# Strassen products in layer 1 of the last two groups, a later start for batch 1's loads, and a written order in place of a list scheduler

## The chip, the cores, the metric

One core of one Trainium2 chip. Times are device microseconds (us) of one execution. The kernel before takes 303.9 us (median of 3 runs, 302.27 to 304.15). It was run again beside every experiment, so each result also has a ratio to runs of the kernel before on the same chip in the same minutes. Runs marked slow (four of experiments, eight of the kernel before, all of these beside c1 to c3) are left out of ratios.

## The reference

Linear attention with cosine weights (8 batches, 8 heads, 576 tokens, head size 64), then a feed-forward part on all 4608 tokens whose gate is h cos h:

```python
def phi(x, c, s):
    r = np.maximum(x, 0.0)
    return np.concatenate([r * c, r * s], axis=-1)
q_p, k_p = phi(q, cos_w, sin_w), phi(k, cos_w, sin_w)
kv = np.einsum('bhsf,bhsd->bhfd', k_p, v)
num = np.einsum('bhsf,bhfd->bhsd', q_p, kv)
den = np.einsum('bhsf,bhf->bhs', q_p, np.sum(k_p, axis=2))[..., None] + 1e-06
x = (num / den).transpose(0, 2, 1, 3).reshape(B * S, H * D)   # 4608 x 512
h = x @ w_in                                                  # 512 x 2048
out = (h * np.cos(h)) @ w_out                                 # 2048 x 512
```

## The kernel before

The 4608 tokens make nine groups of 512: batches 0 to 6, "r" (the fifth tiles of all batches), batch 7. A group goes through layer 1 (products with `w_in`, cosine on ScalarE, gate on VectorE) and layer 2 (products with `w_out`). Layer 2 of all groups but 0 uses Strassen's seven half-size products in place of eight. The kernel describes all work as operations with engines, assumed durations and buffers; a list scheduler orders them on assumed times, and each engine then gets a fixed list.

```python
SQ, DQ, LAND = "SP", "DMA", 2.0                      # assumed: a transfer lands 2.0 us late
def run(self, cold=0.0):                             # the list scheduler
    ...
        t0, e0 = min((c[0], c[1]) for c in cand)
        t, _, us, o, _ = min((c for c in cand if c[1] == e0 and c[0] <= t0 + self.EPS), key=...)
...
# batch 1's loads wait for two quarters of w_out
if b == 1:
    deps.append(w_land[NG + 1])
...
# layer 1, every group: plain, one bank per 512 columns, 4 matmuls of 512
ps[key] = ppool.tile([P, len(js), s1 - s0], F32, name="M1", tag="m1")
...
# layer 2, Strassen, groups 1 to 7 and r: three banks X, Y, Z, five additions on VectorE
e1 = op({"A": 0.6}, EV, lambda e: cp(e, part(g, "s1"), ps[(g, "X")]), deps=[p1], acq=[s1])
p6 = product(1, wsum, S_(1), [sY])
e6 = op({"V": 0.69}, EV, lambda e: add(part(g, "u2"), g, "Y", "s1"), deps=[p6, e1], ...)
...
# layer 2 of group 0: plain, 64 matmuls of 512
layer2_plain(lambda t, n: (1, 1, t, n))
```

The kernel uses eight banks of PSUM, the memory that TensorE's results go to: four in ring "m1", two in "l2", and one tile of two banks, "at", which attention uses for sums over all eight heads.

Names in the profile: `qm`, `km`, `vm` are inputs as loaded, `qp` and `kp` their features phi(q) and phi(k), `V` the values cast to 16 bits; `KV` and `N` are attention's products, `x` its result, `xT` and `TP` transposes; `M` is a bank of layer 1, `ch` the cosine, `g` the gated result; `PX`, `PY`, `PZ` are layer 2's banks X, Y, Z (in the kernel after Y is mostly called `SD`); `s`, `WT`, `WS` are Strassen's sums, `ost` the output.

Of the kernel before, what the change touches and what calls it, by code (L numbers as in the profile page):

```python
# [14 lines left out]

class Slot:


    def __init__(self, ring, n=1):
        self.ring, self.left, self.end = ring, n, 0.0  # L20


def flat(x):
    return tuple(z for y in x for z in flat(y)) if isinstance(x, tuple) else (x,)


class Op:
    def __init__(self, alts, prio, fn, deps, lat, acq, rel, at):
        self.alts, self.prio, self.fn, self.deps, self.lat = alts, flat(prio), fn, deps, lat
        self.acq, self.rel, self.at, self.end = acq, rel, at, None  # L30


class Plan:


    SEM, EPS = 0.08, 0.1

    def __init__(self, rings):
        self.ops, self.free = [], {r: [0.0] * n for r, n in rings.items()}
# [6 lines left out]
    def run(self, cold=0.0):  # L46
        users, wait = {}, {}
        for o in self.ops:
            wait[o] = len(o.deps)
            for d in o.deps:  # L50
                users.setdefault(d, []).append(o)
        ready = [o for o in self.ops if not wait[o]]
        clock, order = {}, []
        while ready:
            cand = []
            for o in ready:
                t = max([o.at] + [d.end + d.lat for d in o.deps])
                if any(not self.free[s.ring] for s in o.acq):
                    continue
                for s in o.acq:  # L60
                    t = max(t, min(self.free[s.ring]))
                for e, us in o.alts.items():
                    cand.append((max(t, clock.get(e, 0.0)), e, us, o, t))
            if not cand:
                left = [(o.prio, o.alts, [s.ring for s in o.acq if not self.free[s.ring]],
                         [(d.prio, d.alts) for d in o.deps if d.end is None][:3])
                        for o in self.ops if o.end is None]
                raise RuntimeError("no operation can start: " + repr(left[:12]))
            t0, e0 = min((c[0], c[1]) for c in cand)
            t, _, us, o, _ = min(  # L70
                (c for c in cand if c[1] == e0 and c[0] <= t0 + self.EPS),
                key=lambda c: (c[4] if e0 == "DMA" else 0.0, c[3].prio, c[0]))
            if e0 == "PE" and t < cold:
                us *= 1.7
            for s in o.acq:
                self.free[s.ring].remove(min(self.free[s.ring]))
            o.end = t + us + (self.SEM if us else 0.0)
            clock[e0] = t + us
            for s in o.rel:
                s.left, s.end = s.left - 1, max(s.end, o.end)  # L80
                if not s.left:
                    self.free[s.ring].append(s.end)
            order.append((t, len(order), o, e0))
            ready.remove(o)
            for u in users.get(o, ()):
                wait[u] -= 1
                if not wait[u]:
                    ready.append(u)
        assert len(order) == len(self.ops)
        order.sort(key=lambda x: x[:2])  # L90
        return [(o, e) for _, _, o, e in order]
# [3 lines left out]
def kernel(  # L95
# [50 lines left out]
    WT = cpool.tile([P, 4, HJ, HM], F16, name="WT")  # L146
# [4 lines left out]
    kvzs, kps, qps, qTs, qTr, x16s, xts, gts, sms, osts, ps = ({} for _ in range(11))  # L151
    T, T1 = range(NT), range(NT + 1)
    HS = [slice(0, HB), slice(HB, H)]
    RING = {"m1": 4, "l2": 2, "at": 1}
# [20 lines left out]
    def feat(eng, b, name, t, g, hs=ALLH):  # L175
        dst = (kps if name == "k" else qps)[b][:, t, hs, g, :]
        src, sc = raw[name][:, hs, t, :], CS[:, b % 2, g, t:t + 1]
        if eng == "A":
            nc.scalar.activation(out=dst, in_=src, func=AF.Relu, scale=sc)  # L179
        else:  # L180
            (nc.vector if eng == "V" else nc.gpsimd).tensor_scalar(  # L181
                out=dst, in0=src, scalar1=0.0, scalar2=sc, op0=ALU.max, op1=ALU.mult)
# [10 lines left out]
    def q_tiles(b):  # L193
        qps[b] = apool.tile([P, NT + 1, H, 2, D], F16, name=f"qp{b}", tag="qp", bufs=1)

    def qT_tiles(b):
        qTs[b] = apool.tile([P, NT, H, P], F16, name=f"qT{b}", tag="qT", bufs=1)

    def qR_tiles(b):
        qTr[b] = apool.tile([P, H, P], F16, name=f"qR{b}", tag="qR", bufs=2)  # L200

    def qT(b, t):
        return qTs[b][:, t] if t < NT else qTr[b]
# [27 lines left out]

    def ratio(b, t, tile_, hbs):
        nb, h0 = len(hbs), hbs[0] * HB
        den = apool.tile([P, nb, HB], F32, name=f"den{b}_{t}", tag="den")
        nc.vector.tensor_scalar_add(out=den, in0=tile_[:, :, :, D], scalar1=1e-6)
        rec = apool.tile([P, nb, HB], F32, name=f"rec{b}_{t}", tag="rec")
        nc.vector.reciprocal(out=rec, in_=den)  # L237
        if hbs[0] == 0:
            x16s[(b, t)] = apool.tile([P, H, D], F16, name=f"x16{b}_{t}", tag="x16", bufs=4)
# [19 lines left out]

    def transposes(key, tag, srcs_, **kw):  # L260
# [4 lines left out]
    def q_src(b, t, h):  # L265
        return qps[b][:, t, h].rearrange("p g d -> p (g d)")

    def q_trans_dma(b, t):
        nc.sync.dma_start_transpose(  # L269
            out=qT(b, t), in_=qps[b][:, t].rearrange("p h g d -> p (h g d)"))  # L270
# [12 lines left out]

    def sin(key):
        ps[("ch", key)] = apool.tile([P, SM], F32, name="ch", tag="ch", bufs=4)
# [4 lines left out]
    def gate(key, dst):  # L290
        m = ps[key]
        nc.vector.tensor_tensor(  # L292
            out=dst, in0=m, in1=ps[("ch", key)].rearrange("p (j s) -> p j s", s=m.shape[2]),
            op=ALU.mult)
# [4 lines left out]
    def s_tiles(g):  # L299
        sms[g] = gpool.tile([P, 2, HJ, HT], F16, name=f"s{g}", tag="s")  # L300

    def sums(g, c, n):
# [3 lines left out]
        a12, s1, s2 = gv[:, 1, js, 0:HT], sms[g][:, 0, js], sms[g][:, 1, js]  # L306
        out, in0, in1, op = ((s1, a21, a22, ALU.add), (s2, s1, a11, ALU.subtract),
                             (a21, a11, a21, ALU.subtract), (a12, a12, s2, ALU.subtract))[n]
        nc.vector.tensor_tensor(out=out, in0=in0, in1=in1, op=op)  # L309

    def weight_sum(n):
        wv = w_out_sb.rearrange("p (j e) m -> p e j m", e=2)
        b11, b12 = wv[:, 0, :, 0:HM], wv[:, 0, :, HM:Dm]
        b21, b22 = wv[:, 1, :, 0:HM], wv[:, 1, :, HM:Dm]
        x, y = ((b12, b11), (b22, WT[:, 0]), (b22, b12), (b21, WT[:, 1]))[n]
        nc.vector.tensor_tensor(out=WT[:, n], in0=x, in1=y, op=ALU.subtract)

    def prod(g, n, c):
        gv = gts[g].rearrange("p (j e) s -> p e j s", e=2)
        sv, wv = sms[g], w_out_sb.rearrange("p (j e) m -> p e j m", e=2)  # L320
        lo, hi, ml, mh = slice(0, HT), slice(HT, SM), slice(0, HM), slice(HM, Dm)
        bank, first, lhs, rhs = (
            ("X", True, gv[:, 0, :, lo], wv[:, 0, :, ml]),
            ("Y", True, sv[:, 1], WT[:, 1]),
            ("X", False, gv[:, 1, :, lo], wv[:, 1, :, ml]),
            ("Y", False, gv[:, 0, :, hi], WT[:, 2]),
            ("Z", True, sv[:, 0], WT[:, 0]),
            ("Y", False, gv[:, 1, :, hi], WT[:, 3]),
            ("Z", False, gv[:, 1, :, lo], wv[:, 1, :, mh]))[n]
        first = first and c == 0  # L330
        if first:
            tag = "m1" if bank == "Z" and g in ALONE else "l2"
            ps[(g, bank)] = ppool.tile(
                [P, 2, HM], F32, name=f"P{bank}", tag=tag, bufs=4 if tag == "m1" else 2)
        for i in range(2):
            for j in range(c * HJ // 2, (c + 1) * HJ // 2):
                nc.tensor.matmul(  # L337
                    ps[(g, bank)][:, i, :], lhsT=lhs[:, j, i * P:(i + 1) * P], rhs=rhs[:, j],
                    start=(first and i == 0 and j == 0), stop=(j == HJ - 1),
                    skip_group_check=True)  # L340

    def part(g, name):
        ps[(g, name)] = apool.tile([P, 2, HM], F32, name=name, tag=name, bufs=1)
# [6 lines left out]
    def add(dst, g, bank, other):  # L350
        nc.vector.tensor_tensor(out=dst, in0=ps[(g, bank)], in1=ps[(g, other)], op=ALU.add)  # L351

    def rows(b):
        ap = out[b * S:(b + 1) * S, :]
        return (ap[0:S5].rearrange("(p t) m -> p t m", t=NT + 1),
                ap[S5:S].rearrange("(p t) m -> p t m", t=NT))

# [13 lines left out]

    def plain2(t, js):
        if js[0] == 0:
            ps[("M2", t)] = ppool.tile([P, Dm], F32, name="M2", tag="l2", bufs=2)
        for j in js:
            nc.tensor.matmul(  # L376
                ps[("M2", t)], lhsT=gts[0][:, j, t * P:(t + 1) * P], rhs=w_out_sb[:, j, :],
                start=(j == 0), stop=(j == NJT - 1))
# [26 lines left out]
    def weights(n):  # L405
# [4 lines left out]
        else:  # L410
# [3 lines left out]
    plan = Plan({"m1": 4, "l2": 2, "at": 1, "raw_k": 1, "raw_q": 1, "raw_v": 1, "kp": 1,  # L414
                 "qp": 1, "V1": 1, "kvz": 3, "qT": 1, "qR": 2, "xT": 2, "x16": 4, "ch": 4,
                 "g": 2, "s": 2, "ld": 2, "s1": 1, "u2": 1, "u3": 1, "ost0": 1, "ost1": 1})
# [380 lines left out]
```

## Time and profile before

| | kernel before |
|---|---|
| time, median of 3 (us) | 303.9 |
| profiled run: its time, the span in its trace (us) | 300.7, 298.7 |
| TensorE, time that its matmuls need | 270.0 |
| holes 23.3 to 67 / 67 to 235 / 235 to end | 2.3 / 9.9 / 0.0 |
| first cosine of layer 1: batch 1 / r / batch 7 (us) | 59.7 / 230.5 / 256.5 |

How to read it: I count a **hole** from the trace's matmul records, as the time from one matmul's start to the next one's, less what the first needs when they stand back to back (216 ns for 512 columns, 109 for 256, 56 for 128, 30 for 65, as the records of the kernel before have them), if over 0.12 us. This is finer than length minus busy time, which the prediction uses: a matmul's record is 0.16 us longer than these spacings (379 ns for 512 columns, 273 for 256) and counts as busy to its end, so each hole looks shorter. "Time that matmuls need" is the recorded number of each size times those spacings. The profile's lines for the kernel before are in the prediction.

### The profile page before, as it was taken

What the parts mean: (1) busy time and instruction counts of PE and PEld (TensorE: products, weight loads), DVE (VectorE), ACT (ScalarE), POOL (GpSimd) and SP (SyncE); (2) the same over time, 40 slices, a digit from 0 to 9 for tenths busy, and PEclk for the clock granted to TensorE, in tenths of its full rate; (3) what the DMA queues carried; (4) which work ended last, traced back from release to release, by engine and by line L of the source; (5) the groups of instructions that cost most, each with busy time, mean ns of one, the idle gap of its engine ahead of it and who ended that gap; (6) DMA issues with size and microseconds to landing.
All of it is one profiled execution on the core that took longest, in us unless ns stands there. A gap on an engine that the chain in (4) does not pass through costs nothing.

```text
span 298.7 us, 6583 instructions
## 1 busy us (share of the span) xinstructions
PE 280.1 (94%) x2565; PEld 201.3 (67%) x2565; DVE 233.7 (78%) x450; ACT 175.6 (59%) x303; POOL 102.0 (34%) x107
## 2 busy tenths in 40 slices
PE   8879999899969987999979999999999999999993
PEld 8768856688855555566646666776666666566782
DVE  1878888899995798887869798987786786768661
ACT  2846748599379797679489497634433443443210
POOL 1370004396191686287077194011002001100500
PEclk9979999999999999999999999999999999999998
DMA  7799995897899999999999999715202100200213
GB/s 218 264 163 203 204 362 183 279 308 120 273 274 235 356 232 169 283 278 203 322 256 202 238 369 195 141 47 151 35 0 94 48 1 32 111 2 0 91 52 140
DMA packets 77086, 53.29 MB, mean 178 GB/s; under 512 B 46080, under 2 KB 74752, under 8 KB 77056
## 3 DMA queue, kind: packets, MB, share of 16 engines
q1 hardware_dynamic: 69760, 39.73, 55.2%
q0 software_dynamic: 6848, 12.59, 16.6%
q10 hardware_dynamic: 448, 0.57, 0.5%
q8 instruction: 20, 0.33, 0.5%
q14 instruction: 10, 0.08, 0.1%
HBM read 36.74 MB, written 9.44 MB: 155 GB/s over the span
## 4 chain that ended last, share of the span: by engine, by line
PE 55%; DMA 16%; DVE 10%; POOL 5%; SPq 5%; ACT 4%; issue 3%; ACTq 0%; DVEq 0%
PE M L279 26%; DMA vm<-in_v_dram 13%; PE PY L337 8%; PE PZ L337 6%; PE PX L337 5%; PE M L376 5%; POOL qp L181 4%; DMA qm<-in_q_dram 3%; PE KV L219 2%; DVE g L292 2%; SPq L171 2%; DVE x L241 2%; PE TP L263 2%; DVE s L309 2%; SPq L269 1%
## 5 line engine op out<-in xcount | busy, mean ns | idle before, releaser
L279 PE MATMUL M<-xT,w_in_sb 128*128 128x512 f16 (+1 forms) x640 | 120.2, 336 | 2.9 <-ACT xT L159 2.6
L286 ACT ACTIVATE ch<-M 128x512 f32<-128x512 f32 x144 | 84.9, 595 | 60.8 <-PE M L279 58.7
L292 DVE TENSOR_TENSOR g<-M,ch 128x512 f16<-128x512 f32 x128 | 85.8, 687 | 27.0 <-ACT ch L286 26.1
L279 PEld LDWEIGHTS <-w_in_sb 128*128 128x128 f16 x704 | 67.3, 98 | 46.6 <-issue 3.1
L181 POOL TENSOR_SCALAR qp<-qm,CS 128x512 f16<-128x512 f32 x29 | 60.0, 2074 | 31.0 <-DMA qm<-in_q_dram 27.0
L337 PEld LDWEIGHTS <-g 128*128 128x128 f16 x560 | 54.1, 98 | 11.5
L369 POOL DMA_DIRECT2D out_dram<-ost x14 | 7.8, 558 | 98.6 <-DVE ost L351 42.5
L179 ACT ACTIVATE kp<-km,CS 128x512 f16<-128x512 f32 x52 | 35.1, 715 | 0.2
L179 ACT ACTIVATE qp<-qm,CS 128x512 f16<-128x512 f32 x40 | 26.9, 713 | 11.9 <-DMA qm<-in_q_dram 11.9
L337 PE MATMUL PX<-w_out_sb,g 128*128 128x256 f16 x224 | 27.6, 273 | 0.0
L241 DVE TENSOR_TENSOR x<-N,rec 128x512 f16<-128x512 f32 (+1 forms) x44 | 26.1, 594 | 1.7 <-DVE rec L237 0.2
L337 PE MATMUL PY<-WT,g 128*128 128x256 f16 x224 | 27.2, 273 | 0.0
L337 PEld LDWEIGHTS <-s 128*128 128x128 f16 x224 | 21.4, 98 | 7.1 <-DVE s L309 2.8
L161 POOL CAST V<-vm 128x512 f16<-128x512 f32 (+1 forms) x22 | 13.9, 664 | 15.9 <-DMA vm<-in_v_dram 15.9
L228 PE MATMUL N<-kvz,qT 128*128 128x65 f16 x256 | 14.7, 196 | 2.3 <-DVE x L241 2.1
L228 PEld LDWEIGHTS <-qT 128*128 128x128 f16 x256 | 12.6, 100 | 6.1 <-issue 3.5
L337 PE MATMUL PY<-WT,s 128*128 128x256 f16 x112 | 14.1, 273 | 2.2 <-DVE s L309 2.2
L181 DVE TENSOR_SCALAR kp<-km,CS 128x512 f16<-128x512 f32 x28 | 15.5, 590 | 0.3 <-DMA km<-in_k_dram 0.2
L292 DVE TENSOR_TENSOR gr<-M,ch 128x512 f16<-128x512 f32 x16 | 10.9, 689 | 5.7 <-ACT ch L286 5.5
L219 PE MATMUL KV<-V,kp 128*128 128x65 f16 x320 | 12.9, 196 | 2.5 <-DVE kp L181 0.7
L279 PE MATMUL M<-xR,w_in_sb 128*128 128x512 f16 x64 | 15.1, 379 | 0.0
L219 PEld LDWEIGHTS <-kp 128*128 128x128 f16 x320 | 11.7, 99 | 4.7 <-issue 2.4
(70 smaller groups left out, 287.7 us busy)
## 6 DMA issues: line engine op xcount, KB each, us to landing
out_dram<-ost POOLq DMA_DIRECT2D x28, 256.0 KB, 4.1
qm<-in_q_dram SPq DMA_DIRECT2D x8, 640.0 KB, 5.3
km<-in_k_dram SPq DMA_DIRECT2D x8, 640.0 KB, 7.0
qm<-in_q_dram SPq DMA_DIRECT2D x8, 512.0 KB, 5.8
km<-in_k_dram SPq DMA_DIRECT2D x8, 512.0 KB, 8.8
vm<-in_v_dram SPq DMA_DIRECT2D x6, 640.0 KB, 8.1
vm<-in_v_dram SPq DMA_DIRECT2D x6, 512.0 KB, 8.9
w_in_sb<-in_moe_w_in_dram POOLq DMA_DIRECT2D x4, 512.0 KB, 9.0
```

What stands on the lines that cost most here:

```text
L161: (nc.vector if eng == "V" else nc.gpsimd).tensor_copy(out=out, in_=in_)
L179: nc.scalar.activation(out=dst, in_=src, func=AF.Relu, scale=sc)
L181: (nc.vector if eng == "V" else nc.gpsimd).tensor_scalar(out=dst, in0=src, scalar1=0.0, scalar2=sc, op0=ALU.max, op1=ALU.mult)
L219: nc.tensor.matmul(tile_[:, n, hh, :], lhsT=kps[b][:, t, h].rearrange("p g d -> p (g d)"), rhs=V1[:, t, h, :], start=(t == 0), stop=(t == NT))
L228: nc.tensor.matmul(tile_[:, n, hh, :], lhsT=qT(p, t)[:, h, :], rhs=kvzs[p][:, h, :], start=(i == 0), stop=(i == len(parts) - 1))
L241: nc.vector.tensor_tensor(out=dst, in0=tile_[:, :, :, 0:D], in1=rec.unsqueeze(3).broadcast_to((P, nb, HB, D)), op=ALU.mult)
L279: nc.tensor.matmul(ps[key][:, n, :], lhsT=w_in_sb[:, c, j * P:(j + 1) * P], rhs=x[:, c, s0:s1], start=(c == 0 and n == 0), stop=(c == NCT ...
L286: nc.scalar.activation(out=ps[("ch", key)], in_=ps[key].rearrange("p j s -> p (j s)"), func=AF.Sin, bias=math.pi / 2.0, scale=1.0)
L292: nc.vector.tensor_tensor(out=dst, in0=m, in1=ps[("ch", key)].rearrange("p (j s) -> p j s", s=m.shape[2]), op=ALU.mult)
L337: nc.tensor.matmul(ps[(g, bank)][:, i, :], lhsT=lhs[:, j, i * P:(i + 1) * P], rhs=rhs[:, j], start=(first and i == 0 and j == 0), stop=(j ...
L369: e0.dma_start(out=five[:, t0:t0 + 2, :], in_=blocks(ost, n))
L376: nc.tensor.matmul(ps[("M2", t)], lhsT=gts[0][:, j, t * P:(t + 1) * P], rhs=w_out_sb[:, j, :], start=(j == 0), stop=(j == NJT - 1))
```

## The change

Its intent: fewer TensorE cycles (Strassen also in layer 1 of r and 7 and in layer 2 of group 0), fewer VectorE additions in layer 2, no waits on late transfers. The diff, cut to its core:

```diff
-    def run(self, cold=0.0):        # the list scheduler
+    def run(self):
+        return [(self.ops[int(x.rstrip("VAG"))], x.lstrip("0123456789"))
+                for x in ORDER.split()]          # a written list: operation, engine
...
-    SQ, DQ, LAND = "SP", "DMA", 2.0
+    SQ, DQ, LAND = "SP", "DMA", 2.5              # slack, used by the search for ORDER
...
-                        deps.append(w_land[NG + 1])
+                        deps.append(w_land[NG + 2])        # three quarters; hold copy likewise
...
+    def bank_tile(g, qd, bank):     # layer 1 by Strassen: quads of banks X, Y, Z
+        if bank != "X" and wide(g, qd):                    # odd quads: Y, Z are
+            if bank == "Z":                                # the halves of one tile
+                t = ppool.tile([P, 2, 512], F32, name="YZ", tag="at", bufs=1)
+                for i, nm in enumerate("YZ"):
+                    ps[(g, qd, nm)] = t[:, i].rearrange("p (i s) -> p i s", i=2)
+        else:
+            ps[(g, qd, bank)] = ppool.tile([P, 2, HT], F32, name=..., tag="m1")
...
+            p1 = mm(0, xs + ys[-1:], [X], rx)
+            p5 = mm(1, [xsum[0], wsum1[0], p1] + ..., [Z], [slot])
+            y1 = op({"A": 0.6, "V": 0.69}, EV, y_seed, deps=[p1, p5], ...)   # Y <- copy of X
+            e5 = op({"A": 0.6, "V": 0.69}, EV, evac5, deps=[p5, ga], acq=[q5])
+            p6 = mm(2, [xsum[1], wsum1[1], y1], [], [slot])                  # adds onto the seed
...
-    layer2_plain(lambda t, n: (1, 1, t, n))
+    layer2(0, lambda i: (1, 1, i))               # Strassen for group 0 too
```

A **seed** is a copy of product 1 that is written into bank Y, onto which later products are then added; two **cover** matmuls write all of banks Y and Z of the "at" tile once before the first seed. A **quad** is a fourth of a group's layer 1. The **hold copy** is a tiny GpSimd copy from the layer-2 weights that makes batch 1's loads wait for them. Layer 2 takes the same form (seed, two additions, five copies). To make room, rings of x and of cosines shrink from 4 to 3 buffers.

> **What bounds the kernel now.** I read the page first (busy shares), then the busy times by stretch, then TensorE's waits, then the timeline of ScalarE around the longest waits.
>
> ```profile
> PE 280.1 (94%) x2565; PEld 201.3 (67%) x2565; DVE 233.7 (78%) x450; ACT 175.6 (59%) x303; POOL 102.0 (34%) x107
> ```
>
> TensorE is busy 94% of the span, so its work plus its holes are the time. The stretches show where the holes are (columns: stretch, length, PE, PEld, DVE, ACT, POOL busy with counts, clock, DMA share, GB/s):
>
> ```profile
> 0.00:16.75 16.75, 13.83 (x186) 12.72 (x186) 9.06 (x22) 9.34 (x15) 5.27 (x15) 0.99 0.71 219
> 16.75:23.30 6.55, 5.30 (x72) 4.68 (x72) 5.24 (x22) 2.50 (x6) 3.53 (x5) 0.77 1.24 205
> 23.30:50.90 27.60, 27.60 (x225) 19.41 (x223) 24.39 (x46) 19.42 (x33) 3.89 (x10) 1.00 1.06 251
> 50.90:60.00 9.10, 7.78 (x132) 6.24 (x129) 6.71 (x30) 5.17 (x12) 2.79 (x3) 1.00 0.76 239
> ...
> 80.00:90.00 10.00, 7.32 (x83) 6.20 (x81) 9.79 (x21) 7.22 (x13) 8.90 (x6) 1.00 1.14 281
> ...
> 110.00:121.00 11.00, 8.45 (x105) 5.92 (x106) 9.09 (x17) 8.42 (x15) 5.78 (x4) 1.00 1.07 177
> ...
> 140.00:158.00 18.00, 15.81 (x172) 10.56 (x171) 13.71 (x29) 12.15 (x22) 8.11 (x6) 1.00 1.06 270
> ...
> 191.00:280.80 89.80, 89.80 (x648) 60.11 (x647) 67.69 (x112) 36.19 (x61) 8.78 (x16) 1.00 0.16 51
> ```
>
> Length minus PE is the hole. Up to 23.3 us the kernel waits for its first inputs (much of PE there is dummies). Then: 1.3 us at 50.9 to 60, and, with the stretches left out, 8.3 us between 80 and 191 (2.7 + 0.4 + 2.5 + 2.2 + 0.3 + 0.2). From 191 to 281 there is none: inputs are in, DMA nearly silent, TensorE alone sets the pace. After its last matmul (294.0) come 4.7 us of last addition and store. Who ended the holes:
>
> ```profile
> PE N L228 <- DVE x L241: 2.8, 2, 2.1
> PE M L279 <- ACT xT L159: 2.6, 1, 2.6
> PE PY L337 <- DVE s L309: 2.2, 2, 1.6
> ```
>
> These name the last releaser, not the cause. ScalarE ahead of the first and third long hole:
>
> ```profile
> 88.75 0.63 ACT L159 ACTIVATE V<-vm 128x512 f16<-128x512 f32 x1 [1.80 <-DMA vm<-in_v_dram]
> 89.28 0.58 ACT L159 ACTIVATE xT<-TP 128x512 f16<-128x512 f16 x1
> ...
> 150.81 0.72 ACT L179 ACTIVATE qp<-qm,CS 128x512 f16<-128x512 f32 x1 [2.98 <-DMA qm<-in_q_dram]
> 151.43 0.58 ACT L286 ACTIVATE ch<-M 128x512 f32<-128x512 f32 x1
> ```
>
> Each time ScalarE stood 1.8 to 3.0 us before an instruction of a later batch whose load had not landed; the copy or cosine that TensorE needed was queued behind it. VectorE passes it on (its gate at 152.0 waited 3.5 us for that cosine). The hole at 109 to 115 is VectorE: a queue of attention divisions and sums (starts about 0.61 us apart) ahead of the sum that the product waits for. So these holes come from a fixed order that counted on transfers landing earlier than they do, and on a full VectorE.
>
> [...]a chain piece of 20 matmuls of 512 columns took 4.32 us (216 ns each), 16 of 256 took 1.75 us (109 ns).[...]the sums of g took 0.68 us with GpSimd idle (111.48) but 1.10 and 0.98 us while GpSimd cast V and made features (112.09, 113.22).[...]
>
> **The change, part by part.**
>
> 1. Strassen in layer 1 of the last two groups (the fifth tiles "r", and batch 7). Plain: 64 matmuls of 512, 64 x 0.216 = 13.8 us. New: 4 quads x 7 products x 4 matmuls of 256 = 112, x 0.109 = 12.25 us. Saves 1.57 us a group, 3.15 us for two, in a stretch with no holes, so at face value. The cover costs 2 x 0.216 = 0.43 us. Weight loads (98 ns) still hide under 109 ns.
> 2. Group 0's layer 2 becomes Strassen too: 64 of 512 to 112 of 256, again 1.57 us. But here TensorE waits for batch 1: KV at 50.9 starts as soon as the values are cast. I count nearly all of it as hidden, turning into a longer hole before batch 1's layer 1. It also puts eight sums (8 x 0.7 = 5.6 us) on VectorE in an already tight stretch.
> 3. Vector work in layer 2: five additions a group before (5 x 0.69) become two, and five copies on ScalarE or VectorE; many of the 28 + 16 denominator additions (156 ns) may move to ScalarE. VectorE loses about 1.8 us a group at its 0.61 us spacing. Counting the suffixes of the order list in the diff: 412 V, 346 A, 83 G; with two instructions for each of 44 divisions about 456 on VectorE, as before (450), and some 45 more on ScalarE (x 0.6 = 27 us on an engine with 120 us free).
> 4. Vector work of the new layer 1: a group gets 8 additions (8 x 0.61 = 4.9 us) and 4 half-size fp16 sums (about 0.4 each), 6.5 us, and 8 PSUM copies on ScalarE. A pass of the late stage has 18.9 us VectorE busy in 26 us. New: 18.9 - 1.8 + 6.5 = 23.6 us against 12.25 + 12.25 = 24.5 us of TensorE, and one pass also holds a 1.2 us weight sum. So VectorE becomes nearly co-bound in the last 50 us. I charge 1.0 us of new holes.
> 5. Batch 1's loads wait for three quarters of the layer-2 weights. Before, they began at 33.9 us, and the weights' last quarter landed by 38.9. DMA is saturated there (share 1.06), so bytes only change places: weights earlier, batch 1's first load about 2.5 us later, its last about the same. I charge 0.5 us.
> 6. The order, searched with longer transfer times. This aims at the 8.3 us of holes between 80 and 191. TensorE has backlog enough: batch 7 is in by 191, its layer 1 starts at 255. So the holes are order, not bandwidth. I expect three quarters to go: 6.3 us.
> 7. The tail: the last product is split in two halves with 128 KB stores; about 0.4 us.
>
> Sum from the profiled run (300.7 us measured, span 298.7): 300.7 - 3.15 + 0.43 + 1.0 + 0.5 - 6.3 - 0.4 = 292.8. The three timed runs before had a median of 303.9, over the profiled one, which I take for more late transfers of the same kind. An order with slack should suffer less; I add 0.7 and say **293.5 us** as the median, 3.4% faster.
>
> **Rivals.** (a) The holes are DMA bandwidth: share above 1.0 from 80 to 191, value loads up to 12 us to land. Then an order can't remove them, and only parts 1 and 7 remain: about 301, same. Against: no hole after 191 and a 50 us lead of batch 7. (b) VectorE becomes the bound: in the late stage its 23.6 us is a count with no waits, and each quad has a chain product, copy, product, addition, product, addition. If it stalls 2 to 3 us a pass, the late stage gains nothing: about 296.5. The sums of group 0 could open holes of 2 us at 40 to 60 too. (c) The order works fully and group 0's saving counts: holes after 23.3 us shrink to 3 in all; TensorE 261 - 4.3 = 257 us, plus 23.3, plus 4.3 tail, plus 2 outside the span: 289.
>
> **Range and chances.** (c) gives the low end, 289.5; (b) with half the holes left gives the high end, 298.5. Faster by over 2% means under 297.8; that takes some 60% of the holes gone or a mix of lesser gains. Faster 0.83, same 0.16, slower 0.01.
>
> **What would show each step.** Right: TensorE busy falls to about 276 us; holes between 80 and 191 fall from 8.3 to about 2; no ScalarE wait on qm or vm of 2 us just ahead of a cosine or xT copy; group r and 7 layer 1 are 112 matmuls each near 109 ns apart; a hole of 2 to 4 us near 45 to 60 us; VectorE over 85% in the last 50 us with TensorE holes under 2 us there. Wrong: holes of the same size elsewhere (rival a), TensorE waiting on VectorE or on seeds at the end (rival b), or the early stage ending more than 2 us later than now.

## The result, and the profile after

After: **307.65 us** (median of 4 runs, 306.6 to 308.26); before, beside it, 303.8 (302.27 to 304.15, 4 runs). The ratio is **1.0133**, 95% interval 1.0089 to 1.0177: 1.3% slower. All runs are fast ones, results are correct. (A ratio here is the mean time of one kernel's fast runs over that of the other's of the same rounds, so not quite the ratio of the medians.) The prediction, 293.5 with a range to 298.5, was wrong.

| profiled runs (us) | before | after | difference |
|---|---|---|---|
| time that matmuls need | 270.0 | 265.6 | -4.4 |
| holes 23.3 to 67 | 2.3 | 8.7 | +6.4 |
| holes 67 to 235 | 9.9 | 10.25 | +0.3 |
| holes 235 to end | 0.0 | 5.0 | +5.0 |
| span | 298.7 | 306.5 | +7.8 |

The products became as cheap as predicted. The holes took it back more than twice over, early and late; in the middle, where the order was to gain 6.3 us, nothing changed in sum. The page of the kernel after:

```profile
PE 280.1 (91%) x2711; PEld 215.7 (70%) x2711; DVE 248.9 (81%) x459; ACT 190.1 (62%) x348; POOL 115.4 (38%) x114
```

Busy TensorE stayed at 280.1, where I expected 276: after a pause the last matmul's end is drawn 0.16 us longer, and there are 19 more pauses, which makes up about 3 of the 4 us. Busy times by stretch of the kernel after, columns as in the prediction:

```profile
23.30:50.90 27.60, 24.00 (x225) 20.46 (x223) 23.31 (x41) 17.95 (x32) 2.51 (x5) 1.00 1.07 240
50.90:60.00 9.10, 7.26 (x110) 6.21 (x108) 8.66 (x19) 7.53 (x15) 6.25 (x9) 1.00 0.28 85
...
140.00:158.00 18.00, 16.66 (x161) 11.77 (x159) 16.19 (x29) 11.39 (x21) 8.67 (x9) 1.00 0.94 208
...
180.00:205.00 25.00, 22.78 (x215) 15.84 (x212) 19.38 (x36) 15.60 (x29) 12.25 (x9) 1.00 1.15 250
...
235.00:300.00 65.00, 62.23 (x557) 54.23 (x555) 52.23 (x84) 35.21 (x62) 7.67 (x14) 1.00 0.11 41
```

The first stretch, without a hole before, now lacks 3.6 us. The last lacks 2.8 us with VectorE at 80% (52.23 of 65) and DMA nearly silent (share 0.11): nothing from outside holds TensorE there. Its waits between 67 and 235 us:

```profile
PE M L323 <- DVE qp L215: 2.0, 1, 2.0
PE M L323 <- DMA xT<-x: 1.5, 2, 1.0
PE SD L434 <- DVE SD L195: 1.3, 1, 1.3
PE PX L434 <- ACT ost L193: 1.3, 1, 1.3
...
PE SD L434 <- DVE s L336: 0.4, 1, 0.4
```

Of the three old waits only the third is left, as `SD <- DVE s`, with 0.4 us in place of 2.2. New ones came.

### Where the late holes come from

The timeline of the kernel after around one of them (start, length, engine, line, operation, in brackets the idle time before it and what ended it):

```profile
253.65 0.60 PE L379 MATMUL YZ<-xsr,WS 128*128 128x256 f16 x4
...
254.28 0.58 ACT L193 ACTIVATE YZ<-M 128x512 f32<-128x512 f32 x1 [0.22 <-PE YZ L379]
...
254.90 0.60 ACT L193 ACTIVATE p<-YZ 128x512 f32<-128x512 f32 x1
...
255.54 0.60 PE L379 MATMUL YZ<-xsr,WS 128*128 128x256 f16 x4 [0.42 <-ACT p L193]
```

At 253.65 product 5 fills bank Z. At 254.28 ScalarE writes the seed into bank Y, at 254.90 it copies Z to SBUF. Product 6 (255.54) adds onto Y. Besides Strassen's sums, the kernel's own list of dependencies names only the seed, done at 254.86; but product 6 started 0.04 us after the copy of **Z** had ended, another bank. In the built program I resolved each wait to the instruction that releases it: 18 waits between instructions on this tile (it is made four times) join accesses that touch different halves. The framework in which the kernel is written orders accesses by tile here, and Y and Z of the odd quads are one tile. The search for the order had one of these waits, the seed's for product 5 (`deps=[p1, p5]`), but not the others.

### Where the early holes come from

By place, the 8.7 us are: 1.1 in layer 1 of group 0, 3.5 in layer 2 of group 0, 2.5 at batch 1's K times V, 1.6 in the rest of its attention. The kernel before had 2.3, all in the last place. The longest waits, from 23.3 to 67 us:

```profile
PE PY L434 <- DVE PZ L336: 1.2, 1, 1.2
...
PE KV L251 <- ACT kp L213: 1.0, 1, 1.0
PE PX L434 <- ACT p L193: 0.7, 1, 0.7
```

The first and third are hand-overs of the new layer 2 of group 0: an addition, and the copy of X, that the next product waits for. With a gate (0.8 us) and a sum (0.5) they make the 3.5 us. Note also that 1.6 us of the 6.4 new ones are the hidden saving itself: TensorE has that much less to do before batch 1 arrives. The second wait is K times V.

Batch 1's attention starts with K times V, in which every feature of K and every cast value takes part. ScalarE's features and GpSimd's casts of batch 1, before:

```profile
45.50 1.95 ACT L179 ACTIVATE kp<-km,CS 128x512 f16<-128x512 f32 x3
```

```profile
47.18 0.90 POOL L161 CAST V<-vm 128x256 f16<-128x256 f32 x2 [0.68 <-DMA vm<-in_v_dram]
48.73 1.25 POOL L161 CAST V<-vm 128x256 f16<-128x256 f32 x3 [0.66 <-DMA vm<-in_v_dram]
```

and after:

```profile
47.94 3.77 ACT L213 ACTIVATE kp<-km,CS 128x512 f16<-128x512 f32 x6
```

```profile
49.53 6.59 POOL L195 CAST V<-vm 128x256 f16<-128x256 f32 x8 [11.23 <-DMA vm<-in_v_dram]
```

Before, VectorE made six of the ten features and GpSimd five of the casts, done at 50.0. The written order gives ScalarE eight features and GpSimd eight casts, 0.82 us each in place of 0.43, done at 56.1. The last value landed at 50.9 (before 48.6), so at most 2.3 of the 6.1 us by which casts and features end late are the load. Layer 1 of batch 1 starts 5.7 us late (65.4 against 59.7).

### The middle: a wait with the wrong name

The longest wait is put down to VectorE's `qp`. The timeline says otherwise (SPq is SyncE issuing transfers; then VectorE; then TensorE):

```profile
187.75 3.63 SPq L207 DMA_DIRECT2D vm<-in_v_dram  x1
191.47 4.68 SPq L686 DMA_TRANSPOSE xT<-x  x2
197.06 3.21 SPq L313 DMA_TRANSPOSE qT<-qp  x2
200.36 2.97 SPq L686 DMA_TRANSPOSE xT<-x  x2
```

```profile
199.72 0.69 DVE L280 TENSOR_TENSOR x<-N,rec 128x512 f16<-128x512 f32 x1 [0.51 <-DMA xT<-x]
```

```profile
206.13 1.24 PE L323 MATMUL M<-xT,w_in_sb 128*128 128x512 f16 x5 [2.03 <-DVE qp L215]
```

Batch 7's six loads were issued from 184.1 to 187.7; two transposes of x, issued at 191.5, landed at 199.6 and 200.1 only, 8.1 us later for the first (2.4 us when the queue is empty, at 216 to 226 us). The last x waited for a buffer that such a transpose still read (199.72), its own transpose was issued at 201.7 and landed at 206.04; TensorE went on at 206.13.

### The profile page after: what moved, and what is told of

It is laid out like the page before. It is cut to its first block, busy times and chain, and to the rows that moved or that the text cites. A ratio compares the mean times of both kernels' runs of the same rounds, so it can differ in the third digit from the quotient of the medians.

```text
span 306.5 us, 6942 instructions
## 1 busy us (share of the span) xinstructions
PE 280.1 (91%) x2711; PEld 215.7 (70%) x2711; DVE 248.9 (81%) x459; ACT 190.1 (62%) x348; POOL 115.4 (38%) x114
## 3 DMA queue, kind: packets, MB, share of 16 engines
q1 hardware_dynamic: 69920, 39.86, 55.1%
## 5 line engine op out<-in xcount | busy, mean ns | idle before, releaser
L323 PE MATMUL M<-xT,w_in_sb 128*128 128x512 f16 (+1 forms) x576 | 107.5, 334 | 4.1 <-DVE qp L215 2.0
L385 ACT ACTIVATE ch<-M 128x512 f32<-128x512 f32 x124 | 72.7, 596 | 48.0 <-PE M L323 33.1
L323 PEld LDWEIGHTS <-w_in_sb 128*128 128x128 f16 x576 | 54.6, 99 | 36.2 <-issue 4.1
L434 PEld LDWEIGHTS <-g 128*128 128x128 f16 x640 | 61.9, 98 | 16.4 <-issue 5.8
L215 POOL TENSOR_SCALAR qp<-qm,CS 128x512 f16<-128x512 f32 x19 | 40.1, 2116 | 54.4 <-DMA qm<-in_q_dram 43.4
L215 POOL TENSOR_SCALAR kp<-km,CS 128x512 f16<-128x512 f32 x14 | 29.3, 2094 | 1.6 <-DMA km<-in_k_dram 1.6
L434 PEld LDWEIGHTS <-s 128*128 128x128 f16 x256 | 24.5, 98 | 6.9 <-issue 1.6
L213 ACT ACTIVATE kp<-km,CS 128x512 f16<-128x512 f32 x38 | 25.8, 712 | 3.7 <-DMA km<-in_k_dram 3.7
L215 DVE TENSOR_SCALAR qp<-qm,CS 128x512 f16<-128x512 f32 x20 | 12.1, 611 | 5.9 <-DMA qm<-in_q_dram 5.9
L251 PE MATMUL KV<-V,kp 128*128 128x65 f16 x320 | 13.6, 196 | 3.5 <-ACT kp L213 1.0
L434 PE MATMUL PZ<-WT,s 128*128 128x256 f16 x128 | 16.4, 273 | 0.0
L434 PE MATMUL PZ<-w_out_sb,g 128*128 128x256 f16 x128 | 16.3, 272 | 0.0
L434 PE MATMUL SD<-WT,s 128*128 128x256 f16 x112 | 14.5, 272 | 1.8 <-DVE SD L195 1.3
```

Of the source, the lines that this page charges most:

```text
L213: nc.scalar.activation(out=dst, in_=src, func=AF.Relu, scale=sc)
L215: (nc.vector if eng == "V" else nc.gpsimd).tensor_scalar(out=dst, in0=src, scalar1=0.0, scalar2=sc, op0=ALU.max, op1=ALU.mult)
L251: nc.tensor.matmul(tile_[:, n, hh, :], lhsT=kps[b][:, t, h].rearrange("p g d -> p (g d)"), rhs=V1[:, t, h, :], start=(t == 0), stop=(t == NT))
L323: nc.tensor.matmul(ps[key][:, n, :], lhsT=w_in_sb[:, c, j * P:(j + 1) * P], rhs=x[:, c, s0:s1], start=(c == 0 and n == 0), stop=(c == NCT ...
L385: nc.scalar.activation(out=ps[("ch", key)], in_=ps[key].rearrange("p j s -> p (j s)"), func=AF.Sin, bias=math.pi / 2.0, scale=1.0)
L434: nc.tensor.matmul(ps[(g, bank)][:, i, :], lhsT=lhs[:, j, i * P:(i + 1) * P], rhs=rhs[:, c * HJ // 2 + j], start=(first and i == 0 and j = ...
```

## The experiments

Eighteen kernels ran. Theories: **O**, the written order is at fault, the old scheduler would do better; **L**, late loads of batch 1 make the early holes; **C**, VectorE's sums for group 0 do; **H**, waits between the two banks of one tile make the late holes; **S**, the seeds make the middle holes; **D**, late inputs do; **F**, the order on the engines itself does. Medians are of all runs, holes of the profiled run from 23.3 us on (what is lost before that is not in them).

| run | median us | ratio to before (95%) | holes early / middle / late |
|---|---|---|---|
| after | 307.65 | 1.0133 (1.0089 to 1.0177) | 8.7 / 10.25 / 5.0 |
| e1_half_wait | 309.09 | 1.0201 (1.0121 to 1.0281) | 8.9 / 9.6 / 5.0 |
| e2_ws_late | 307.79 | 1.0128 (1.0056 to 1.0201) | 7.65 / 8.65 / 5.0 |
| e3_both | 306.21 | 1.0096 (1.0055 to 1.0136) | 6.9 / 9.8 / 5.0 |
| e4_x16 | 309.2 | 1.0196 (1.0152 to 1.024) | 9.2 / 10.2 / 5.0 |
| g1_greedy | 314.76 | 1.0367 (1.0295 to 1.044) | 8.8 / 9.5 / 10.95 |
| g2_no_l1 | 314.82 | 1.0337 (1.0266 to 1.0409) | 8.4 / 16.4 / 1.8 |
| g3_no_l1_l2 (wrong result) | 307.79 | 1.0113 (1.0011 to 1.0215) | 5.95 / 13.6 / 1.7 |
| g4_no_l2 (wrong result) | 319.84 | 1.0528 (1.0448 to 1.0609) | 6.65 / 11.35 / 10.95 |
| h1_two_tiles | 303.28 | 0.9951 (0.988 to 1.0022) | 8.7 / 8.8 / 1.1 |
| h2_two_tiles_e3 | 301.75 | 0.9902 (0.9814 to 0.9991) | 6.8 / 10.2 / 1.1 |
| h3_plain_late | 310.26 | 1.0177 (1.0093 to 1.0261) | 9.1 / 10.3 / 1.75 |
| s1_seed_free (wrong result) | 309.66 | 1.0156 (1.0089 to 1.0224) | 8.7 / 10.25 / 5.0 |
| d1_after_noload (wrong result) | 300.05 | 0.9891 (0.9724 to 1.0058) | 8.9 / 2.2 / 5.0 |
| d2_before_noload (wrong result) | 294.12 | 0.9696 (0.955 to 0.9841) | 3.15 / 3.4 / 0.0 |
| f1_no_sums0 (wrong result) | 307.81 | 1.0147 (0.9972 to 1.0322) | 8.05 / 11.1 / 5.0 |
| c1_reordered | 299.77 | 0.9881 (0.9823 to 0.9938) | 6.2 / 7.3 / 0.9 |
| c2_slack | **296.44** | **0.978** (0.9728 to 0.9831) | 5.4 / 3.1 / 0.7 |
| c3_slack | 300.93 | 0.993 (0.9903 to 0.9958) | 4.7 / 3.8 / 1.35 |

### Early: loads, sums, engines

e1 undoes part 5 of the change:

```diff
-                                in_=w_out_sb[0:2, (NG - 2) * NJT // NG, 0:1])
+                                in_=w_out_sb[0:2, (NG - 3) * NJT // NG, 0:1])
```

> Undoes one part of the change alone: batch 1's loads wait for two quarters of the layer-2 weights, not three. In the changed kernel they start at 37.6 us against 33.9 before, and batch 1's layer 1 runs without breaks from 63.7 us against 58.9. Theory L (the late loads are a good part of the 4.8 us lost up to there): loads start near 35, features of q at 42.5 in place of 44.4, layer 1 of batch 1 near 61.5, total 2 us less, about 305.6. Theory V (vector work of the new layer 2 of group 0 sets the pace there): features of q earlier, but the values and keys of batch 1 done as late as now, layer 1 of batch 1 within 0.7 us of 63.7, total within 0.7 us of 307.6.

The last value landed 1.2 us sooner (49.7), early holes stayed at 8.9: **L fell** as the main cause.

e2 moves the three sums of the input weights, 1.2 to 1.4 us of VectorE each, from 49 to 54.5 us to the 200s:

```diff
- ... 273G 196V 214 ... 272G 197V 256A ... 257A 198V 219A ...      (in ORDER)
+ ... 1206V 196V ... 772V 197V ... 799V 198V ...
```

> Moves only the three sums of the layer-1 weights (1.25 us each on VectorE, at 49 to 54 us in the changed kernel) to idle places of VectorE at 187, 206 and 222 us; nothing needs them before 238. Theory V: keys and values of batch 1 come off VectorE and GpSimd earlier (GpSimd's casts of V fall from 0.82 us towards 0.45[...]), the last KV product of batch 1 ends near 55 in place of 57.3, total 1.5 to 2 us less, about 306. Theory L: ScalarE's queue of keys (ends at 54.6) holds it, and it gains under 0.7 us.

Early holes fell by 1.05 us; the time did not change clearly. GpSimd's eight casts, no longer beside these sums, were done at 53.1 in place of 56.1:

```profile
49.69 3.40 POOL L194 CAST V<-vm 128x256 f16<-128x256 f32 x8 [11.55 <-DMA vm<-in_v_dram]
```

So the 0.82 us of a cast (0.43 here, for as many) came from the sums of the input weights, not from the number of casts. But ScalarE's features still ended at 54.3, and K times V then waited 1.5 us for them.

e3 has both edits and gives seven features and casts other engines:

```diff
- 258A 256A 255A 275G 274G 277G 279A
+ 258V 256V 255V 275A 274V 277V 279V
```

> Both edits, and seven features of batch 1 moved between engines (three keys and two value casts to VectorE, two casts to and from ScalarE), so that no engine holds more than its share. If L and V together are the early loss: layer 1 of batch 1 without breaks from about 59.5 us, total about 4 us less, 303.5. Rival (later holes are set by when transfers are issued, so an earlier start is given back): layer 1 of batch 1 earlier by 3 us or more but total only 1 to 1.5 us less.

Early holes fell to 6.9, the time to 306.2. Those at K times V fell from 2.5 to 0.9; those in layer 2 of group 0 stayed at 3.6. The intervals of e3 and after overlap, so only the profile shows a gain.

f1 takes the opposite side, VectorE's sums (the sums of g of group 0 and all sums of the output weights are skipped, the products read plain blocks):

```diff
+        if g == 0:
+            return                                    # sums of g, group 0
...
-        nc.vector.tensor_tensor(out=dst, in0=x, in1=y, op=ALU.subtract)     # weight sums
```

> WRONG RESULT on purpose. The kernel after without the eight sums of group 0's g and without the eight sums of the output weights (16 VectorE instructions of about 0.7 us, 11 us in all, of which most stand between 33 and 58 us); the products read plain blocks of g and of the weights in their place, as many and as large. Theory C (the early 6.4 us of new holes are VectorE and what queues behind it, crowded by group 0's Strassen layer 2): holes from 23 to 67 us fall from 8.7 to 4 us or less, layer 1 of batch 1 starts about 4 us sooner than at 65.4. Rival L (batch 1's values arrive too late, at 50.9 us, and cast on GpSimd): holes stay above 6.5 us, layer 1 of batch 1 at 64 or later.

Early holes fell by 0.65 us only, layer 1 of batch 1 started at 65.3: **C fell**. The waits for sums went, but TensorE then waited 1.1 us for a landing of the output weights, and the hand-overs through the copy of X and through Z stayed. With 11 us of VectorE work gone, VectorE stood idle while ScalarE still made its eight features, until 55.1, and GpSimd its eight casts, until 56.2: in fixed lists nobody takes over. So of the 6.4 us the runs show e3's part, 1.8 us, where features and casts are. The 3.5 us in layer 2 of group 0 are read from the waits of the trace; no run isolates them. In g3 below, where that layer is plain, one hole of 1.5 us stands there; in c2, whose new order has no hole at K times V, 4.4 of its 5.4 us still do (1.8 of these wait for the output weights).

### The order against the scheduler, and x's ring

e4 gives x four buffers again (`zero` is put into a tile that is unused until then, for room):

```diff
-"x16": 3
+"x16": 4
```

> Gives the x tiles (attention's result ahead of the transposing DMA) four buffers as before, in place of three; 1 KB found by laying the warm-up zeros into a tile not yet used. Theory B (VectorE stands in its queue for an x buffer that a transpose of 6 to 8 us still reads; the chain that ended last runs over two such transposes, 166.2 to 172.2 and 191.5 to 199.6): the wait of VectorE on the transpose is gone, the holes at 172 and 204 shrink from 2.5 us to under 1, total 1.5 to 2.5 us less, about 305.5. Rival (the transposes are late themselves, behind the loads in the queue): holes stay, total within 0.7 us of 307.6.

No gain: the wait for a buffer in the 200s was itself made by late transposes.

The next four use the operations of the kernel after with the list scheduler of the kernel before; g2 to g4 take parts away (Strassen in layer 1, in layer 2 of group 0, or both):

```diff
-        for o, e in plan.run():                # g1: ORDER
+        for o, e in plan.run():                # g1: the scheduler of the kernel before
-    STR = {"r", 7}                             # g2, g3
+    STR = set()
-    layer2(0, lambda i: (1, 1, i))             # g3, g4
+    layer2_plain(lambda t, n: (1, 1, t, n))
```

> The changed program with all its new operations, but ordered by the list scheduler of the kernel before in place of the written order[...]. Theory O (the written order is at fault; the new operations are sound): 299 to 303, below the changed kernel's 307.6 by 5 us or more. Rival W (the new operations cost more than the 4.3 us of TensorE time that they save, under any order): 306 or more.

> As g1_greedy, without Strassen in layer 1 of the last two groups (nor its weight sums, cover matmuls and 12 KB). Under W with the layer-1 part as the cost: 2 us or more faster than g1_greedy. If that part gives what its matmul count says: 2.7 us slower than g1_greedy.

> As g2_no_l1, and layer 2 of group 0 plain as before; what is left of the change are the PSUM seeds in layer 2, finer buffers and more freedom of engines. If the early vector work is the cost: 1.5 us or more faster than g2_no_l1; if the saving of 1.57 us there is simply hidden: within 0.7 us; should the seeds and buffers alone be dear, it stands at 304 or more.

> As g1_greedy with layer 2 of group 0 plain, Strassen in layer 1 kept: tells whether the two parts add. Additive: g1_greedy plus the difference of g3_no_l1_l2 and g2_no_l1, within 1 us.

**O fell**: on the same operations the written order is 2.3% better than the scheduler (1.0133 against 1.0367). All of that is late (5.0 against 10.95 us of holes); up to 235 us the two lose about the same (19.0 and 18.3). The four times do not add up (taking layer 2 of group 0 away costs 5 us with Strassen in layer 1 and gains 7 without), so a scheduler's choices hide a part's worth, and these runs are weak evidence on parts. One thing they do show: late holes are 10.95 us with Strassen in layer 1 and under 2 without. (g3 and g4 compute wrong results: a sum overwrites a block of the output weights before the plain layer 2 reads it. Their instructions are the same.)

### Late: one tile of two banks

h1 keeps order, banks and instructions, and makes Y and Z two tiles:

```diff
-                t = ppool.tile([P, 2, 512], F32, name="YZ", tag="at", bufs=1)
                 for i, nm in enumerate("YZ"):
-                    ps[(g, qd, nm)] = t[:, i].rearrange("p (i s) -> p i s", i=2)
+                    t = atpool[0].tile([P, 512], F32, name=f"W{nm}", tag=f"at{i}", bufs=1)
+                    ps[(g, qd, nm)] = t.rearrange("p (i s) -> p i s", i=2)
```

(the two-bank pool of attention is closed when attention is done, and one with two tags opened on the same banks)

> The kernel after, same written order, one edit: in the odd quads of layer 1 of the last two groups the banks Y and Z are two tiles of one bank each, in place of the two halves of one tile of two banks. In the program as built, 18 waits between instructions on that one tile are between accesses that touch different halves (product 6, which writes Y, waits for the copy that reads Z; product 7 waits for the cosine that reads Z); with two tiles these waits are gone. Theory H (these waits between different banks make most of the 5.0 us of TensorE holes after 235 us): holes after 235 us fall to about 1.5 to 2.5, the time by 2.5 to 3.5 us, to about 304.5. Rival E (the engines themselves are the limit there, VectorE 80 to 85% busy; the wait only changes its name): holes after 235 us stay above 4, time within 1 us of the kernel after's 307.6.

**H holds**: late holes 5.0 to 1.1, time 1.8% below the kernel after (0.9951 against 1.0133), results correct. (In the profiled run 1.4 us of middle holes went too, where nothing was edited; the edit's own part is the 3.9 us.) The same place in the kernel h1:

```profile
250.78 0.60 PE L386 MATMUL WZ<-xsr,WS 128*128 128x256 f16 x4
251.04 0.59 ACT L197 ACTIVATE WY<-M 128x512 f32<-128x512 f32 x1
...
251.55 0.59 ACT L197 ACTIVATE p<-WZ 128x512 f32<-128x512 f32 x1
...
252.09 0.60 PE L386 MATMUL WY<-xsr,WS 128*128 128x256 f16 x4
```

Two things changed: the seed (251.04) no longer waits for product 5, and product 6 (252.09) starts before the copy of Z has ended (252.14), with no idle time ahead of it.

> h1's edit on top of e3's (two quarters instead of three, weight sums later, seven casts moved). Late and early holes are separate stretches, so if H holds the two gains add: 307.6 - 1.4 (e3) - 3 = about 303.2, level with the kernel before. If H falls: 306, as e3.

h2 (h1's and e3's edits, diffs above) adds the two gains: 301.75, clearly better than the kernel after, and better than the kernel before by 1% (interval to 0.9991).

h3 keeps the written order up to r's layer 1 and goes on with plain layer 1 under the scheduler:

```diff
-    STR = {"r", 7}
+    STR = set()
...
+        for o, e in toks: ... place(o, e)      # PREFIX: ORDER up to r's layer 1
+        # then the list scheduler
```

> The kernel after with its written order kept up to the first instruction of layer 1 of group r (about 237 us; instruction by instruction the same on all engines, the sums of the input weights included though unused), then plain layer 1 for r and 7 and everything left, ordered by the list scheduler of the kernel before. Theory (part 1 of the change is worth about nothing as written, its 3.15 us of saved products less 0.43 of cover come back as 5.0 us of holes; a plain late stage has about 1.8 us of holes, as in g2): 307.6 - 5.0 + 1.8 + 2.7 = 307.1, so within 1 us of the kernel after. If part 1 does save what was predicted: about 310. If it costs: under 306.

The profiled run is as expected (span 306.2 against 306.5); in time h3 is 0.4% slower than the kernel after, with overlapping intervals, so the times alone do not decide. By the counts, Strassen in layer 1 saves 2.7 us of products (3.15 less the cover) and has 5.0 us of holes as written, 1.1 in h1. The kernel before has none there, so against it the part cost 2.3 us as written and gains 1.6 in h1. Against h3's plain late stage, with its 1.75 us of holes, it cost about 0.5 and gains 3.4. The time from r's first layer-1 matmul to the last matmul agrees: before 64.5 us, after 67.6, h3 66.3, h1 63.7, where after and h1 have 0.9 us of the group before's products in it besides.

### Middle: seeds, inputs, order

s1 lets the seed of layer 2 in groups 1 to 6 come from SBUF:

```diff
-                cp(e, ps[(g, "Y")], ps[(g, "X")])
+                cp(e, ps[(g, "Y")], ps[(g, "X")] if g in ("r", 7) else w_in_sb[:, 0, 0:512]...)
```

> WRONG RESULT on purpose. The kernel after, but in layer 2 of groups 1 to 6 the seed of Y is copied from the weights in SBUF instead of from the bank X: same copies on the same engines in the same order, but the seed no longer waits for product 1, and product 2 no longer for the seed. Theory S (the hand-overs through the seed, product 1, copy, products 2 and 6, make 3 us or more of the 10.25 us of holes between 67 and 235 us): middle holes fall to about 7, time by about 3 us to 304.6. Rival D (the middle holes are late transfers and just-in-time attention that turn up at whatever instruction comes next): middle holes stay above 9, time within 1.2 us of 307.6.

Middle holes 10.25, the sum the same to the hundredth as before the edit, though single waits changed: **S fell**.

d1 and d2 leave out six batches' loads, in the kernel after and in the kernel before:

```diff
     def load(b, name, half, hs=ALLH):
+        if b > 1:
+            return
```

> WRONG RESULT on purpose. The kernel after without the loads of q, k and v of batches 2 to 7: their tiles keep the values of batches 0 and 1, so no feature and no value cast waits for a load, and the transfers that are left (transposes, stores, weights) have the DMA engines nearly to themselves. Same order on every engine. Theory D (the 10.25 us of holes between 67 and 235 us are late inputs: loads and, behind them, the transposes of x): they fall to 3 us or less and the time by about 7 us, to about 300.5. Rival F (the written order itself: chains of instructions on the engines that stand too close together, whatever the transfers do): the waits on transposes of x (4.0 us of the holes) shrink, the others stay, holes 6 us or more, time down by 4 us or less.

> WRONG RESULT on purpose. The kernel before without the loads of q, k and v of batches 2 to 7, as the run before this. In the kernel before 7.6 of the 9.9 us of holes between 67 and 235 us stood behind ScalarE waiting for a load. If that reading is right they go with the loads: holes in that stretch about 2 to 3 us, time down by about 7 us, to about 296. If the holes stay, the reading of the prediction was wrong already for the kernel before.

**D holds, F fell**: middle holes 10.25 to 2.2 and 9.9 to 3.4. In d1 the waits of TensorE from 67 to 228 us are these two:

```profile
PE SD L436 <- DVE PZ L338: 0.6, 1, 0.6
PE M L325 <- DMA xT<-x: 0.5, 1, 0.5
```

The engine waits (`SD`, `ost`) of the kernel after were echoes of late inputs. d1's time fell by about 7 us; its one round is too few for a close ratio, the holes are what counts.

Is that bandwidth, or order? c1 to c3 take h2's operations and search the order again, with instruction durations from the traces and a single server for transfers fitted to their landings. c1 was searched with transfers slowed by up to 14%, c2 and c3 by 3 to 20% after c1 had shown its own late landings. Their diff is ORDER alone (c1 gives 154 operations another engine).

> h2's program (two tiles for Y and Z, loads of batch 1 behind two quarters) with the written order searched again, starting from h2's: same operations and buffers, other positions in the order and, for 154 copies, features, sums and additions, another of the engines that the change allows. The search used a model of its own with what the traces of this case show in place of assumed durations: the median of each instruction's form on each engine, GpSimd 25% slower than that, one server for all transfers whose service and latency were fitted to the landings of three traces (a load 1.4 to 2.0 us each after 4 to 6 us, a transpose of x 0.8 after 2.4, a store 1.1 after 2.3), slowed by 0, 7, 10 and 14% and with random noise drawn again and again. The model puts h2 at 294 to 304 us of span without noise (measured 300.4) and this order at 285.5 to 287, with noise 290. Theory D (the middle holes are late inputs, which an order built on the real landings can avoid): holes from 67 to 235 us fall from about 10 to 4 or less, early ones to 5 or less, time 289 to 295, over 2% faster than the kernel before. Rival B (the transfers' bandwidth is the limit, so no order helps): middle holes stay above 8, time 299 or more.

> As c1 (h2's program in another order), searched again from h2's order with what c1 showed: features on VectorE 25% and sums 8% longer, GpSimd 10% longer, service of the transfers fitted anew with c1's landings and slowed by 3 to 20% with more noise. In this harsher model c1 has a span of 306 to 310 with noise, this order 297 to 301. Theory (what c1 left between 67 and 235 us, 7.3 us, is again transfers and VectorE instructions slower than the model had them): middle holes 5 or less, time 295 to 298, ratio to the kernel before 0.97 to 0.98. Rival (an order in fixed lists cannot follow transfers that vary from run to run, however it is searched): middle holes about 7, ratio about 0.988 as c1.

> The same search and model as c2_slack, started from c1's order instead of h2's; in the harsher model within 0.5 us of c2_slack. It tells how much of a difference between c1 and c2 is luck of one order: if the theory holds both are at a ratio of 0.97 to 0.98, if only one is, the model does not rank orders that finely.

c2 is **296.44 us, ratio 0.978**, 2.2% faster than before (0.9728 to 0.9831, so faster for certain, by 2% not for certain), results correct. It carries the change's products, and TensorE's busy time reaches the 276 that I had predicted for the change:

```profile
PE 276.5 (94%) x2711; PEld 215.4 (74%) x2711; DVE 243.8 (83%) x473; ACT 182.9 (62%) x335; POOL 111.8 (38%) x113
```

TensorE's waits in it, 60 to 235 us:

```profile
PE M L329 <- DMA xT<-x: 2.0, 1, 2.0
PE M L329 <- DVE g L342: 0.3, 1, 0.3
```

The same bytes move and the middle holes are 3.1, so bandwidth is not the limit; the order is. One difference is in the transfers' queue: after issues batch 7's six loads in a row, from 184.1 to 187.7, c2 spreads them from 174.2 to 193.7 with transposes of x between them, and its transposes of x land after 3.8 us at the median (6.1 in after). No run tests this difference alone.

c3, from the same search and rated within 0.5 us of c2, ran 1.5% slower (span 297.5 against 292.9), though its holes from 23.3 us on are only 0.6 us more. Most of the difference lies before that:

```profile
24.46 1.04 PE L328 MATMUL M<-xT,w_in_sb 128*128 128x256 f16 x4 [3.60 <-DMA w_in_sb<-in_moe_w_in_dram]
```

c3's order issues the third quarter of the layer-1 weights ahead of the first (`4G 9G 5G 7G` in ORDER, c2 has `4G 5G 7G 9G`), so layer 1 of group 0 starts at 24.5 us in place of 20.7. The model had not counted that: it gets most of the gain and does not rank orders to a per cent.

## Why the prediction was wrong, by its own steps

1. **Part 1, layer 1 by Strassen: -3.15 and +0.43.** Right: matmul time fell by 4.4 us in the records for all Strassen parts, and three groups of 1.57 less 0.43 are 4.3.
2. **Part 4, "I charge 1.0 us of new holes". Failed**: 5.0. The reason given (VectorE nearly co-bound) was not it either: with VectorE nearly as full (76% in place of 80%), h1 has 1.1. I took the chain copy, product, addition from the operation list and did not ask what the framework adds for a tile that spans two banks. Rival (b) had the size (2 to 3 us a pass), with the wrong cause.
3. **Part 2, group 0: "nearly all hidden". Failed**: the gain was hidden, but I charged nothing for what it brings, and early holes rose by 6.4 us, 1.6 of them the hidden gain; layer 1 of batch 1 started 5.7 us later. What the step left out is the same as in part 4, the hand-overs of the new form: 3.5 us of holes stand inside layer 2 of group 0. Another 2.5 stand at K times V, behind the features and casts that the new order gives to ScalarE and GpSimd. I had named "holes of 2 us" from sums of group 0; f1 shows that it was not these. How the loss divides is read from the trace; runs show 1.8 us of it (e3).
4. **Part 5, "its last about the same", 0.5 us. Undersized**: the last value of batch 1 landed 2.3 us later, but e1, which undoes part 5, did not gain, so little of it reaches the end.
5. **Part 6, "three quarters to go: 6.3 us". Failed in sum**: 9.9 to 10.25. The reading of the old holes was right (d2: without loads they go), and the old holes did go. What failed is the step from "order, not bandwidth" to "so this order". ORDER was searched with a landing 2.5 us after a transfer's own service; the transposes of x took 6.1 us at the median, and up to 8.3 behind a batch of loads. c2 shows that the step was right about order in principle: 3.1 us are left of 9.9. Holes of the same size elsewhere had been named as the sign of rival (a), bandwidth; they came, but d1 and c2 show that the rival is wrong.
6. **Part 7, tail: -0.4.** Failed by its size: from the last matmul's end to the end of the span 4.8 us before, 4.9 after.
7. **Part 3, VectorE loses 1.8 us a group.** Nearly: its layer-2 additions and copies in groups 1 to 7 and r took 27.5 us before and 16.6 after, 1.4 a group. But its busy time rose by 15.2 us in all, with the new sums and additions and with features of q (12.2 us in place of 5.4). ScalarE's rose by 14.5 where 27 were expected.
8. **Slips that changed little.** The sum of g at 111.48 does not show an idle GpSimd: a cast of V began at 111.52. The sum at 110.88, 0.69 us, does, but for its last 0.04 us or so. Rival (c)'s terms give 289.6, not 289.

With 6.4 + 0.3 + 5.0 of holes added and 4.4 of products saved, the sum is 7.3 us on top of the 300.7 that the profiled run before took: 308.0; the profiled run after took 308.26.

**What the runs show beside it.** The new products of 256 columns stand 109 ns apart (median of their records in the kernel after), with weight loads of 98 ns. Seeds copied by ScalarE and VectorE and then accumulated on give correct results in the kernel after and in h1, h2 and c1 to c3. The cover writes banks Y and Z of the "at" tile before the first seed in that tile; no run leaves it out, so what it is needed for is not shown. h1 is correct without the 18 waits between the two banks: in it ScalarE's seed (251.04 to 251.63) and TensorE's product 5 (250.78 to 251.38) overlap, one on Y, the other on Z.

## What to carry to other kernels

Before charging a chain of engine handovers by its operations, resolve the waits in the built program: two banks in one tile were ordered as one, and splitting the tile took away 3.9 us of holes at the same order. A wait named in a profile can be an echo: take the suspected input away altogether (wrong result on purpose) and see which waits vanish. When an order is searched on a model, check the model's landings against the trace first, by queue and by what stands ahead in it, and look at the start too: c3 lost 3.6 us to the order of its first weight loads.

## Measured here

- Transposes behind loads: in the kernel after a transpose of x landed after 2.4 us with no load ahead of it (four, issued at 215.85 to 226.19) and after up to 8.3 us behind a batch's loads (issued at 133.85). Issuing two of them took SyncE 4.9 us there and 4.7 us at 191.47, where one took 1.2 us at 215.85.
- A tile of two banks: the framework ordered it as one, with 18 waits in the kernel after between accesses to different halves; late holes were 5.0 us, and 1.1 with two tiles (h1).
- VectorE beside GpSimd: features of 512 columns on VectorE took 0.48 us (median) with GpSimd idle in the kernel before and in the kernel after, and 0.70 and 0.62 us with it busy. Casts of 256 columns on GpSimd took 0.43 us before, 0.82 in the kernel after beside VectorE's sums of the input weights, and 0.43 in e2, where these sums stand elsewhere.
